# A gated S5 kernel: the head in two halves, a wider first weight block, and the square root table ahead of the loads

## The chip, the cores and the metric

The kernel runs on one core of a Trainium2 chip. The metric is the device time of one execution, in microseconds (us). The core has five engines that run their own instruction streams and wait for each other at semaphores: PE multiplies matrices (its weight loads are listed as PEld), DVE and ACT and POOL work element by element, and SP only issues transfers (DMAs). ACT and POOL can issue transfers too. A letter q behind an engine's name (SPq, ACTq) means its instruction queue.

## The reference, cut to what matters

The input x has 2048 tokens of 448 features. Two branches share one layer norm and are multiplied at the end.

```python
xn = layernorm(x)                                   # over the 448 features
# branch A: a diagonal complex state space scan over the tokens
dt = exp(log_dt); Lam_bar = exp(dt * Lam)
Bu = xn @ (((Lam_bar - 1) / Lam)[:, None] * Bmat).T
h[t] = Lam_bar * h[t-1] + Bu[t]
s = 2 * real(h @ Cmat.T) + xn * Dskip
# branch B: gated unit, 448 -> 1792 -> 448
hb = sigmoid(xn @ w_gate) * (xn @ w_up)
out = x + s * silu(hb @ w_down)
```

## The kernel before, in words

**Tiling.** The tokens are cut into four chunks of 512, and each chunk into four tiles of 128. Features lie on the partitions for the matmuls: `xnT` holds a chunk of normed tokens transposed, in seven slices of 64 features, doubled so that both halves of the partitions hold what they need. Gate and up weights (`wG`, `wU`) are loaded by halves of the partitions and by blocks of "steps". A chunk has 14 steps, seven of gate and seven of up. Each makes 256 columns (two groups of 128) for the chunk's tokens: seven pairs of matmuls on the upper and lower 64 rows (`gu_mm`, lines 653 and 654), in a `gu` buffer of two PSUM banks. There are three such buffers, used in turn. A gate step is emptied by a tanh on ACT (`gu_evac`, L667), an up step by a multiplication on DVE (L670).

**The scan.** It is turned into real arithmetic with tables of sines and cosines over the position in the chunk. `columns()` (L476) transposes four parameter vectors by small matmuls (L482, L484), copies them out (`pv`, L487), and makes from them `dt` (exp on ACT, L490), `theta` and `turn` on DVE (L499, L502, L504), `arg` (L499 as well) and `r` = exp(`arg`) on ACT (L507). `tables()` (L516) then switches ACT to the table set that has tanh, silu and sine (L518), after `dt` and `r`, and computes for each of four groups of states `v` (L522), `nu` (L525, L527), an absolute value (L530), a sine (L534) and a cosine (L536). Everything from L476 to here is issued in the planner's order, described below.

**The head.** Chunk 0 cannot use the transposes by DMA that the later chunks use, because all starts with it. For each of its tiles: two statistics instructions on DVE (`stats`, L387 and L388), the square root on ACT (L396), a cast of the mean on POOL (L397), the reciprocal (L398) and the norm (L410) on DVE, a copy of 64 columns on POOL (L414); then seven transposes on PE (`pe_transpose`, L439) and a copy to `xnT`: tile 0 by ACT and DVE (L443, L445), tile 1 by ACT (L451), tiles 2 and 3 by DVE (L448). Steps 0, 1 and 2 of gate are computed as tiles come: `g_head(lo, hi)` runs the three steps for tiles lo to hi only, that is with 128 tokens per matmul. The order on PE is that of the program: nine warm-up matmuls on zeros, transposes of tile 0, one warm-up, tile 1, one warm-up, steps 0 to 2 for tile 0, `columns()`, tile 2, the steps for tile 1, tile 3, the steps for tile 2, the steps for tile 3 with the tanhs, and then steps 3 to 13 over all 512 tokens.

**The loads.** SP and ACT issue them in program order (L326): x tiles 0 to 3 alternately, a first block of gate weights with two steps by each of the two queues, two parameter vectors each, on ACT the load of the square root table, then the second block of two steps by each, and on SP both halves of a third block with three steps, x tiles 4 to 7 in one transfer, and the up weights. The statistics of chunk 1 (`stats_for(1)`) read tiles 4 to 7.

**The order of the work.** Every operation is entered in a plan (`add`) with its engine, an assumed cost, and what it reads and writes. `solve` first gives PE's operations due times by adding costs in program order, with the first gate step not due before 5.9. It goes backward from there: each other operation gets a due time from what needs it and from what else its engine has to do. Then it goes forward with a clock of its own: whenever an engine is free, it takes, of the operations that are ready by then, the one with the earliest due time. A load is ready when a model of the transfers says so (all bytes one after another at a fixed rate). The instructions are emitted in the order of these starts, so the order on DVE, ACT and POOL is fixed when the kernel is built. Transfers, and all of PE, keep the program's order.

Of the kernel before, what the change touches and what calls it, by code (L numbers as in the profile page):

```python
# [14 lines left out]
ACT = mybir.ActivationFunctionType  # L15
# [57 lines left out]
class Plan:  # L73
# [8 lines left out]
    def add(self, eng, cost, fn, r=(), w=(), dma=0, lat=None, chain=False, name=""):  # L82
        o = Op()
        o.idx, o.eng, o.cost, o.fn, o.dma, o.name = len(self.ops), eng, cost, fn, dma, name
        o.lat = LAT.get(eng, 0.0) if lat is None else lat
        o.pre, o.suc = {}, []
        o.start = o.end = None
        for k in r:
            if k in self.w:
                self._edge(self.w[k], o, True)  # L90
        for k in w:
            for q in self.r.get(k, ()):
                self._edge(q, o, False)
            if k in self.w:
                self._edge(self.w[k], o, True)
        for k in w:
            self.w[k] = o
            self.r[k] = []
        for k in r:
            if k not in w:  # L100
                self.r.setdefault(k, []).append(o)
        if chain or eng == "PE":
            key = ("chain", eng)
            if key in self.last_of:
                self._edge(self.last_of[key], o, None)
            self.last_of[key] = o
        self.ops.append(o)
        return o
# [114 lines left out]
def kernel(  # L223
# [18 lines left out]
    V, A, G, T, Q = nc.vector, nc.scalar, nc.gpsimd, nc.tensor, nc.sync  # L242
# [8 lines left out]
    def flat(t, *dims):  # L251
        if len(dims) == 1:
            return t
        names = "abcd"[:len(dims)]
        kw = {n: v for n, v in zip(names[1:], dims[1:])}
        return t.rearrange("p (" + " ".join(names) + ") -> p " + " ".join(names), **kw)
# [63 lines left out]
    add = pl.add  # L320
# [3 lines left out]
    def load(eng, key, nbytes, o, i, cost=0.45, r=()):  # L324
        e = {"SP": Q, "ACT": A, "POOL": G}[eng]
        add(eng, cost, lambda: e.dma_start(out=o, in_=i), w=[key] if not isinstance(key, list) else key,  # L326
            r=r, dma=nbytes, chain=True)

    def load_x(t0, n, q="SP", r=()):
        load(q, [("x", t) for t in range(t0, t0 + n)], n * P * D * 2,  # L330
             x_all[:, t0:t0 + n, :], x_src[:, t0:t0 + n, :], r=r)

    BLK = {"g": [(0, 2), (2, 4), (4, 7)], "u": [(0, 3), (3, 7)]}

    def load_w(eng, k, half, b, r=()):
        m0, m1 = BLK[k][b]
        ps = slice(half * H, half * H + H)
        c0 = half * 896
        load(eng, [("w", k, half, m) for m in range(m0, m1)], H * 7 * (m1 - m0) * P * 2,
             wgt[k][ps, :, m0 * P:m1 * P],  # L340
             wsrc[k][:, c0 + m0 * P:c0 + m1 * P].rearrange("(s p) f -> p s f", p=H), r=r)
# [16 lines left out]

    for e in ("SP", "ACT", "POOL"):
        add(e, 0.7, lambda: None, chain=True)  # L360
    for t in range(4):
        load_x(t, 1, ("SP", "ACT")[t % 2])
    load_w("SP", "g", 0, 0)
    load_w("ACT", "g", 1, 0)
    for k, vec in enumerate((A_log_dt, A_Lambda_im, A_Lambda_re, A_Dskip)):
        load("ACT" if k < 2 else "SP", ("vrow", k), D * 2, vrow[k:k + 1, :], vec.unsqueeze(0), cost=0.25)
    add("ACT", 0.3, lambda: A.preload_act_table_set("sqrt_and_others"), w=["sqrttab"], lat=1.0, chain=True)
    load_w("SP", "g", 0, 1)
    load_w("ACT", "g", 1, 1)
    for h in range(2):  # L370
        load_w("SP", "g", h, 2)
    load_x(4, 4)
    for b in (0, 1):
        load_w("SP", "u", 0, b)
# [3 lines left out]
    def warm_mm(n):  # L378
        def f():
            for _ in range(n):  # L380
                T.matmul(gu[2][:, 0, :], lhsT=warm[:, 0:P], rhs=warm[:], start=True, stop=True)
        add("PE", (0.43 if n > 1 else 0.22) * n, f, r=["warm"], w=[("gu", 2)])
# [42 lines left out]
    def next_acc():  # L425
        a = acc_n[0] % 2
        acc_n[0] += 1
        return a
# [4 lines left out]
    def pe_transpose(t):  # L433
        b, a, js = t % NXN, next_acc(), slice(t * P, t * P + P)
        tp = flat(acc[a][:].bitcast(BF16)[:, 0:7 * P], 7, P)

        def f(s0, s1):
            for s in range(s0, s1):
                T.transpose(tp[:, s, :], xn[b][:, s * H:s * H + P], ident[:, :])  # L439
        add("PE", 0.36, lambda: f(0, 6), r=[("xn", b), "ident"], w=[("acc", a)])  # L440
        add("PE", 0.06, lambda: f(6, 7), r=[("xnw", b), ("xn", b), "ident", ("acc", a)], w=[("acc", a)])
        if t == 0:
            add("ACT", 0.476, lambda: A.copy(out=xnT[0][:, 0:4, js], in_=tp[:, 0:4, :]),  # L443
                r=[("acc", a)], w=[("xnT", 0, t, "a")])
            add("DVE", 0.27, lambda: V.tensor_copy(out=xnT[0][:, 4:7, js], in_=tp[:, 4:7, :]),  # L445
                r=[("acc", a)], w=[("xnT", 0, t, "b")])
        elif t > 1:
            add("DVE", 0.53, lambda: V.tensor_copy(out=xnT[0][:, :, js], in_=tp[:, :, :]),  # L448
                r=[("acc", a)], w=[("xnT", 0, t, "a"), ("xnT", 0, t, "b")])
        else:  # L450
            add("ACT", 0.9, lambda: A.copy(out=xnT[0][:, :, js], in_=tp[:, :, :]),  # L451
                r=[("acc", a)], w=[("xnT", 0, t, "a"), ("xnT", 0, t, "b")])
# [9 lines left out]
    def xr(c, lo=0, hi=TPC):  # L462
        return [("xnT", c % 3, j, h) for j in range(lo, hi) for h in "ab"]
# [174 lines left out]
    def next_gu():  # L638
        a = gu_n[0] % 3
        gu_n[0] += 1  # L640
        return a
# [3 lines left out]
    def gu_mm(c, k, m, a, lo, hi, first):  # L645
        x = xnT[c % 3]
        ts = slice(lo * P, hi * P)
        w_ = wgt[k]
        ms = slice(m * P, m * P + P)

        def f():
            for s in range(7):
                T.matmul(gu[a][:, 0, ts], lhsT=w_[0:H, s, ms], rhs=x[0:H, s, ts], start=(s == 0), stop=(s == 6))  # L653
                T.matmul(gu[a][:, 1, ts], lhsT=w_[H:P, (s + 1) % 7, ms], rhs=x[H:P, s, ts],  # L654
                         start=(s == 0), stop=(s == 6))
        n = (hi - lo) * P
        return add("PE", 7 * (0.0028 + n / 2400.0) + (2 * SW if first else 0), f,
                   r=xr(c, lo, hi) + [("w", k, 0, m), ("w", k, 1, m)], w=[("gu", a)], name=f"{k}{c}.{m}")
# [3 lines left out]
    def gu_evac(c, k, m, a):  # L662
        b = m % NSIG
        th, tk = (hF[1][:, m, :, :], ("hF", 1, m)) if c == 0 else (sig[b][:], ("sig", b))
        ho, hk = hF[c % 2][:, m, :, :], ("hF", c % 2, m)
        if k == "g":
            add("ACT", act(1024), lambda: A.activation(th, gu[a][:], ACT.Tanh, scale=0.5),  # L667
                r=[("gu", a)], w=[tk])
        else:
            add("DVE", dve1(1024), lambda: V.scalar_tensor_tensor(out=ho, in0=th, scalar=1.0, in1=gu[a][:],  # L670
                                                                 op0=ALU.add, op1=ALU.mult),
                r=[("gu", a), tk], w=[hk])
# [203 lines left out]
        norm(t)  # L876
    slots0 = [next_gu() for _ in range(3)]

    def g_head(lo, hi):
        for m in range(3):  # L880
            gu_mm(0, "g", m, slots0[m], lo, hi, m == 0)

    pe_transpose(0)
    warm_mm(1)
    pe_transpose(1)
    warm_mm(1)
    g_head(0, 1)
    columns()
    pe_transpose(2)
    g_head(1, 2)  # L890
    pe_transpose(3)
    g_head(2, 3)
    for m in range(3):
        gu_mm(0, "g", m, slots0[m], 3, 4, False)
        gu_evac(0, "g", m, slots0[m])
    b_load()
    def stats_for(c):
# [133 lines left out]
```

## Time and profile before

| what | value |
|---|---|
| median of three executions | 196.55 us (195.38 to 196.55) |
| the profiled execution | 195.65 us, of which span 193.9 us |
| granted PE clock, mean | 0.999 |
| busy: PE, DVE, ACT, POOL | 183.2, 161.8, 85.3, 38.6 us |
| transfers over the whole span | 13.31 MB, mean 69 GB/s |

The span runs from the first to the last instruction that the profiler records; the rest of an execution's time lies around it. A line of the profile names engine, line of the kernel, operation and tiles, with start and length in us. "Idle before" in square brackets is the time in which the engine did nothing, and behind the arrow stands what ended it. "Issue" is waiting for which the profile shows no cause. The chain of waits starts from the last instruction and is followed back, at each step to what released it. Matmuls overlap, so their lengths add up to more than the time that they take; the distance between their starts tells the pace.

### The profile page before, as it was taken

The page shows a single profiled execution, that of the slowest core. Times are in us where ns is not written, and L with a number is a line of the kernel's source. Part 1 is how long each engine was busy: PE and PEld are TensorE (multiplying, and loading weights), DVE is VectorE, ACT ScalarE, POOL GpSimd, SP SyncE. Part 2 cuts the span into 40 slices and gives each one's busy share as a digit, 9 for nine tenths or more (in the row PEclk, how much of TensorE's full clock was granted, in tenths as well). Part 3 has the DMA queues.
Part 4 walks back from the last instruction along what each step waited for, and adds up shares of the span by engine and source line. Part 5 has one row for each costly group of instructions (what it writes and reads, how often), then busy time and mean ns, then how long its engine had stood idle before and what let it go on. Part 6 is the DMA issues. An engine that isn't in the chain of part 4 may idle for free.

```text
span 193.9 us, 3710 instructions
## 1 busy us (share of the span) xinstructions
PE 183.2 (94%) x1482; PEld 91.3 (47%) x1489; DVE 161.8 (83%) x280; ACT 85.3 (44%) x120; POOL 38.6 (20%) x90
## 2 busy tenths in 40 slices
PE   7796999999999999999999999999989999999992
PEld 2583554444454454444445444444435444555561
DVE  3789678799999899999999999999997999540044
ACT  2757991745968652144467232334146421111110
POOL 4376843000008730000666100000000000000000
PEclk9999999999999999999999999999999999999999
DMA  5899975599300033200033410000000001010002
GB/s 140 220 249 222 127 166 74 112 333 206 111 0 0 3 71 78 44 0 0 0 31 93 98 44 3 24 0 27 24 24 0 3 0 46 9 45 24 0 26 70
DMA packets 30025, 13.31 MB, mean 69 GB/s; under 512 B 19636, under 2 KB 30008, under 8 KB 30008
## 3 DMA queue, kind: packets, MB, share of 16 engines
q1 hardware_dynamic: 28788, 12.39, 29.7%
q10 hardware_dynamic: 1220, 0.69, 1.4%
q8 instruction: 11, 0.18, 0.4%
q14 instruction: 6, 0.05, 0.1%
HBM read 6.66 MB, written 1.84 MB: 44 GB/s over the span
## 4 chain that ended last, share of the span: by engine, by line
DVE 49%; PE 33%; issue 6%; DMA 4%; POOL 3%; ACT 3%; ACTq 0%; DVEq 0%; POOLq 0%
PE gu L653 13%; DVE hF L670 11%; DVE wv L759 9%; PE acc L843 6%; PE gu L820 5%; PE acc L820 4%; DVE ta L752 3%; DVE tb L753 3%; DVE z L755 3%; DMA wG<-in_B_w_gate_dram 2%; DVE hT L776 2%; DVE ta L773 2%; DVE tb L774 2%; DVE o_t L856 2%; DVE wv L791 2%
## 5 line engine op out<-in xcount | busy, mean ns | idle before, releaser
L653 PE MATMUL gu<-xnT,wG 64*128 64x512 bf16 (+1 forms) x259 | 47.1, 324 | 2.7 <-issue 1.2
L654 PE MATMUL gu<-xnT,wG 64*128 64x512 bf16 (+1 forms) x259 | 47.2, 325 | 0.0
L653 PE MATMUL gu<-xnT,wU 64*128 64x512 bf16 x196 | 46.1, 376 | 0.0
L654 PE MATMUL gu<-xnT,wU 64*128 64x512 bf16 x196 | 46.1, 376 | 0.0
L667 ACT ACTIVATE sig<-gu 128x1024 f32<-128x1024 f32 x21 | 21.5, 1022 | 37.4 <-PE gu L654 37.4
L820 PE MATMUL acc<-wd,hF 128*128 128x448 bf16 x168 | 33.8, 353 | 0.0
L820 PEld LDWEIGHTS <-hF 128*128 128x128 bf16 x224 | 21.5, 98 | 21.3 <-issue 2.1
L653 PEld LDWEIGHTS <-wG 64*128 64x128 bf16 x259 | 20.8, 94 | 21.7 <-issue 2.5
L653 PEld LDWEIGHTS <-wU 64*128 64x128 bf16 x196 | 18.0, 94 | 23.0 <-issue 2.1
L670 DVE SCALAR_TENSOR_TENSOR hF<-sig,gu 128x1024 bf16<-128x1024 f32 x21 | 25.3, 1208 | 0.8 <-PE gu L654 0.8
L843 PE MATMUL acc<-cT,hT 128*128 128x448 bf16 x105 | 24.3, 353 | 0.0
L759 DVE TENSOR_TENSOR_SCAN wv<-c_r,st,z 128x512 bf16<-128x512 f32 x18 | 22.9, 1277 | 0.0
L856 DVE TENSOR_TENSOR o_t<-acc,g_t 128x448 bf16<-128x448 f32 x15 | 9.2, 616 | 16.3 <-PE acc L843 16.3
L654 PEld LDWEIGHTS <-wG 64*128 64x128 bf16 x259 | 20.5, 94 | 2.9 <-issue 2.7
L716 ACT CAST bus<-gu 128x1024 bf16<-128x1024 f32 x12 | 12.1, 1008 | 13.5 <-PE gu L705 10.9
L654 PEld LDWEIGHTS <-wU 64*128 64x128 bf16 x196 | 18.0, 94 | 0.0
L705 PE MATMUL gu<-xnT,bT 128*128 128x512 bf16 x65 | 15.3, 379 | 1.1 <-issue 1.1
L401 POOL TENSOR_SCALAR veb<-mv 128x2 bf16<-128x2 bf16 x6 | 4.2, 693 | 52.0 <-DVE st L769 27.4
L843 PEld LDWEIGHTS <-hT 128*128 128x128 bf16 x119 | 10.4, 98 | 7.3 <-issue 0.4
L826 ACT ACTIVATE g_t<-acc 128x448 bf16<-128x448 f32 x12 | 6.5, 540 | 14.8 <-PE acc L820 14.7
L387 DVE BATCH_NORM_STATS2 bst<-x_all 128x6 f32<-128x448 bf16 x16 | 9.5, 615 | 2.6 <-DMA x_all<-in_A_x_dram 2.6
L820 PE MATMUL gu<-wd,hF 128*128 128x448 bf16 x56 | 10.8, 352 | 0.0
(131 smaller groups left out, 244.5 us busy)
## 6 DMA issues: line engine op xcount, KB each, us to landing
out_dram<-o_t SPq DMA_DIRECT2D x15, 112.0 KB, 1.7
wd<-in_B_w_down_dram SPq DMA_DIRECT2D x1, 1568.0 KB
x_all<-in_A_x_dram SPq DMA_DIRECT2D x3, 448.0 KB, 5.0
wU<-in_B_w_up_dram SPq DMA_DIRECT2D x2, 448.0 KB, 11.3
wG<-in_B_w_gate_dram SPq DMA_DIRECT2D x2, 336.0 KB, 5.1
wU<-in_B_w_up_dram SPq DMA_DIRECT2D x2, 336.0 KB
wG<-in_B_w_gate_dram SPq DMA_DIRECT2D x2, 224.0 KB, 4.8
wG<-in_B_w_gate_dram ACTq DMA_DIRECT2D x2, 224.0 KB, 4.7
```

Of the source, the lines that this page charges most:

```text
L387: add("DVE", 0.53, lambda: V.bn_stats(out=bst[b][:], in_=x_all[:, t, :]), r=[("x", t)], w=[("bst", b)])
L653: T.matmul(gu[a][:, 0, ts], lhsT=w_[0:H, s, ms], rhs=x[0:H, s, ts], start=(s == 0), stop=(s == 6))
L654: T.matmul(gu[a][:, 1, ts], lhsT=w_[H:P, (s + 1) % 7, ms], rhs=x[H:P, s, ts], start=(s == 0), stop=(s == 6))
L667: add("ACT", act(1024), lambda: A.activation(th, gu[a][:], ACT.Tanh, scale=0.5), r=[("gu", a)], w=[tk])
L670: add("DVE", dve1(1024), lambda: V.scalar_tensor_tensor(out=ho, in0=th, scalar=1.0, in1=gu[a][:], op0=ALU.add, op1=ALU.mult), r=[("gu", a) ...
L705: T.matmul(gu[a][:, i, :], lhsT=bT[:, kt, i, pt * P:pt * P + P], rhs=x[:, 2 * kt, :], start=False, stop=(kt == 2))
L716: add("ACT", act(1024), lambda u=u, a=a: A.copy(out=bus[u][:], in_=gu[a][:]), r=[("gu", a)], w=[("bus", u)])
L759: dve(1.194, lambda k=k: V.tensor_tensor_scan(out=wv[:, k, :], data0=rb, data1=z[:, k, :], initial=(st[pt][:, k, :] if c else 0.0), op0=AL ...
L820: T.matmul(d, lhsT=hF[c % 2][:, m, h, js], rhs=wd[:, ft, :], start=(ft == 0), stop=(ft == FT - 1))
L826: add("ACT", act(448), lambda: A.activation(g_t[g][:], d, ACT.Silu, scale=0.5), r=[key, "silutab"], w=[("gt", g)])
L843: T.matmul(y, lhsT=hT[c % 2][:, hm, js], rhs=cT[:, cm, c0:c1], start=(i == 0), stop=(i == 6))
L856: add("DVE", dve1(n), lambda od=od, y=y, c0=c0, c1=c1: V.tensor_tensor(out=od, in0=y, in1=g_t[g][:, c0:c1], op=ALU.mult), r=[key, ("gt", g ...
```

## The change

Three edits, all in the head.

1. The blocks of the gate weights become (0, 3) and (3, 7) instead of (0, 2), (2, 4) and (4, 7). The loads of the third block go. The second block of each half is still issued by SP and ACT respectively, now with four steps.
2. The load of the square root table is entered ahead of all transfers, directly behind the start of ACT's chain, with an assumed cost of 0.05 and a latency of 1.5 (before: behind two parameter vectors, 0.3 and 1.0).
3. `g_head` goes. Steps 0, 1 and 2 are computed for tiles 0 and 1 together (256 tokens per matmul), with the transposes of tile 2 behind step 0, those of tile 3 behind step 1, and `columns()` between these and step 2. Then the three steps are computed for tiles 2 and 3 together, each with its tanh.

```diff
-    BLK = {"g": [(0, 2), (2, 4), (4, 7)], "u": [(0, 3), (3, 7)]}
+    BLK = {"g": [(0, 3), (3, 7)], "u": [(0, 3), (3, 7)]}
...
+    add("ACT", 0.05, lambda: A.preload_act_table_set("sqrt_and_others"), w=["sqrttab"], lat=1.5, chain=True)
     for t in range(4):
         load_x(t, 1, ("SP", "ACT")[t % 2])
     load_w("SP", "g", 0, 0)
     load_w("ACT", "g", 1, 0)
     for k, vec in enumerate((A_log_dt, A_Lambda_im, A_Lambda_re, A_Dskip)):
         load("ACT" if k < 2 else "SP", ("vrow", k), D * 2, vrow[k:k + 1, :], vec.unsqueeze(0), cost=0.25)
-    add("ACT", 0.3, lambda: A.preload_act_table_set("sqrt_and_others"), w=["sqrttab"], lat=1.0, chain=True)
     load_w("SP", "g", 0, 1)
     load_w("ACT", "g", 1, 1)
-    for h in range(2):
-        load_w("SP", "g", h, 2)
     load_x(4, 4)
...
-    def g_head(lo, hi):
-        for m in range(3):
-            gu_mm(0, "g", m, slots0[m], lo, hi, m == 0)
-
     pe_transpose(0)
     warm_mm(1)
     pe_transpose(1)
     warm_mm(1)
-    g_head(0, 1)
+    gu_mm(0, "g", 0, slots0[0], 0, 2, True)
+    pe_transpose(2)
+    gu_mm(0, "g", 1, slots0[1], 0, 2, True)
+    pe_transpose(3)
     columns()
-    pe_transpose(2)
-    g_head(1, 2)
-    pe_transpose(3)
-    g_head(2, 3)
+    gu_mm(0, "g", 2, slots0[2], 0, 2, True)
     for m in range(3):
-        gu_mm(0, "g", m, slots0[m], 3, 4, False)
+        gu_mm(0, "g", m, slots0[m], 2, 4, False)
         gu_evac(0, "g", m, slots0[m])
```

## The prediction

> **What bounds the kernel now.** I read the busy shares first, then the waits of the matrix engine (PE), then the chain of waits. The first two:
>
> ```profile
> PE 183.2 (94%) x1482; PEld 91.3 (47%) x1489; DVE 161.8 (83%) x280; ACT 85.3 (44%) x120; POOL 38.6 (20%) x90
> ```
>
> ```profile
> PE gu L653 <- issue: 1.2, 1, 1.2
> PE gu L381 <- DVE warm L347: 1.2, 1, 1.2
> ...
> PE gu L695 <- DVE hF L670: 0.6, 1, 0.6
> PE gu L653 <- ACT hF L667: 0.5, 1, 0.5
> ```
>
> PE is busy 94% of the span, and the only waits it has after 18.05 us are 0.6, 0.3 and seven switches of 0.16 us. What PE loses or gains before then moves the end by nearly the same amount. So I ask when PE starts gate step 3, the first with no part in the head. The chain of waits from 9.4 us on (start, length, what):
>
> ```profile
> 9.44 0.16 PE acc L482 x3
> 9.59 0.12 PE acc L484 x2
> 9.71 0.51 PE acc L439 x7
> ...
> 10.25 0.62 DVE xnT L448
> 10.88 0.08 DVE c_theta L499
> ...
> 12.37 0.08 DVE c_arg L499
> ...
> 12.47 0.20 ACT c_r L507
> ...
> 12.69 1.28 ACT L518
> ...
> 13.99 0.63 ACT spm L534
> 14.62 0.92 ACT hF L667
> ...
> 15.58 0.37 PE gu L653
> ```
>
> The reader should see that the head's matmuls are not what is late. Steps 0 to 2 fill all three `gu` buffers; step 3 needs the first one emptied by a tanh (L667), that needs the table load L518, that waits for `c_r` = exp(`c_arg`), and `c_arg` comes from `columns()`. The head's own matmuls end at 15.06. PE then waits 0.5 us, runs five of step 3's seven pairs, and stands still for 1.22 us in mid-step, waiting for nothing that the profile shows. The vector engine (DVE) around `c_arg`, in order of time:
>
> ```profile
> 12.28 0.15 DVE L499 TENSOR_TENSOR c_arg<-c_dt,pv 128x4 f32<-128x4 bf16 x1
> 12.40 0.74 DVE L527 SCALAR_TENSOR_TENSOR hT<-hT,hT 128x513 f32<-128x513 f32 x1
> 13.06 0.61 DVE L448 COPY xnT<-acc 128x896 bf16<-128x896 bf16 x1
> 14.13 1.15 DVE L387 BATCH_NORM_STATS2 bst<-x_all 128x6 f32<-128x448 bf16 x2 [0.46 <-DMA x_all<-in_A_x_dram]
> 15.20 0.30 DVE L388 BATCH_NORM_AGGREGATE mv<-bst 128x2 bf16<-128x6 f32 x2
> 15.42 1.12 DVE L387 BATCH_NORM_STATS2 bst<-x_all 128x6 f32<-128x448 bf16 x2
> ```
>
> `c_arg` stands before the four statistics of chunk 1, the first of which waits for the load of x tiles 4 to 7 until 14.13.
>
> **What the Trainium skill says.** (1) "Runtime: NRT & Kernel Launch", Instruction fetch mechanics: instructions are refilled in blocks of 16 KiB, 256 instructions, by a DMA queue of the sequencer. The trace agrees: queue q8 moves 11 packets, 0.18 MB. One is recorded at 15.2 us, beside loads that keep the DMA engines over 90% busy. I read the 1.22 us as a late block; that is an inference. (2) "TensorE: Matmul & The Clock Gate", Part 1: an array idle for a window of about 3.4 us drops to half clock, and needs about as long to recover; the windows are free-running. The trace shows the first half: nine warm-up matmuls 0.43 us apart, later pairs of the same width 0.216 apart. No gap of that length occurs after the warm-up (the longest is 0.9 us, before 6.10). (3) Same page and part: DVE is a strict FIFO. The trace agrees: the copy of tile 3 (13.06) follows the table operations though its transposes ended at 11.98. (4) "ScalarE: Activation LUTs", What ACT_TABLE_LOAD costs: 1283 ns, plus a drain of 1380. The trace shows 1.28 and no drain: the square root starts 0.02 after the load.
>
> **The change part by part.**
>
> *Square root table first.* The load leaves 3.74 to 5.02 us and lies ahead of the x loads. `mv` of tile 0 is there at 4.12, so the first reciprocal can follow `mv` of tile 1 at 4.77 instead of 5.37: norms and transposes of tiles 0 and 1 come 0.6 us earlier. ACT's queue now has it ahead of x1, x3, wG, two vectors and wG. Price: between 0.2 us (in the trace the next DMA issue follows the load's start by 0.20) and 1.28 (if issue waited for its end); not below zero, as nothing before it leaves. I take 0.2. It is hidden by the next item, as would be most of 1.28.
>
> *Weight block of three.* The first halves grow from 229 to 344 KB each. The old first blocks landed at 6.5, the second at 8.8 (wait of 0.41 ending 8.87): 459 KB in 2.3 us, 200 GB/s, so 229 KB more land at 7.65. The 0.41 goes. SP issues two DMAs less (0.62 each). The x load of tiles 4 to 7 follows the same bytes as before but larger pieces (768 and 1024 B instead of 512 and 768 B). Its bounds: 14.1 as now; 12.6, where DVE gets to it (below). wG in 512 and 768 B pieces moved 2065 KB from 1.9 to 12.0 us, 204 GB/s; wU in the larger ones runs at about 220 (13 to 15 us), which is 0.7 us less. I take 13.4.
>
> *The head.* Tile 1's copy (L451, 0.89) can end at 7.9; PE step 0 over 256 tokens runs 7.95 to 8.72 (seven pairs at 0.11, half of 0.216), transposes of tile 2 to 9.25, step 1 to 9.97, tile 3 to 10.5, `columns()` to 10.8, step 2 to 11.55, the second half 3 x 0.77 to 13.85. That is 1.2 us before the old 15.06, and 84 matmuls with 84 weight loads fewer. Worth nothing by itself: the tanh decides.
>
> *`columns()` moved behind tile 3 and step 1.* It ends at 10.8 instead of 9.7. DVE then copies tile 3 (10.55 to 11.17) and `pv` (11.3); `dt` 11.57, `theta` 11.6, `turn` twice, `v` of pair 0 at 12.15 to 12.6. Now the order. DVE's order is written by the planner: of the operations ready in its own clock the one with the earliest due time. Its numbers decide order alone; no time here is taken from them. Worked out of the kernel before by its rules, the due times are: statistics of tiles 4, 5 at 12.34, 12.87; `theta` 13.73, `v` 14.03, `nu` 14.43; statistics of 6, 7 at 14.83, 15.36; `c_arg` 15.89. Before, `columns()` was early enough that all of the `theta` group was placed (9.64 to 10.84 in planner time) ahead of x tile 4's landing there, 11.77. After, planner `theta` comes at 11.35 and `v` at 11.65, so at 12.05 the statistics are ready and more urgent. The new DVE order is `v`, statistics 4 and 5, `nu`, statistics 6 and 7, **then** `c_arg`. I worked this by hand from the listed costs; it is the step on which the forecast stands. Queued behind the first of them on DVE: everything to `c_arg`; who waits: `c_r`, table load, all tanh, PE.
>
> With x landing at T: statistics 4 and 5 with their aggregates 1.29 (14.13 to 15.42), `nu` 0.34, statistics 6 and 7 1.1, `c_arg` 0.15: T + 2.9. `c_r` 0.2, table 1.28: T + 4.4. The planner then takes tanh before the sine (due 10.3 against 21.2), 1.05 to PE's start: **T + 5.45**. For T = 13.4 PE starts step 3 at 18.85, 3.27 later than 15.58.
>
> *The late block.* The old stall came 20 PE instructions (five pairs, each two matmuls and two weight loads) behind the head. The head has 168 fewer, so that place in the stream moves 188 instructions, 47 pairs, 10.2 us of work, behind step 3's start, and PE has idled meanwhile: the block has time to come. I book −1.22; bounds −1.22 and 0.
>
> *Sum.* +3.27 − 1.22 = +2.05. On the way PE's waits of 0.6 and 0.3 could shrink, DVE's start of the scan waits for PE (1.66 us idle before 35.17), and chunk 1's transposes land about 36.5 against a need at 39.3, so neither absorbs nor adds. The profiled execution took 195.65 us (span 193.9 and 1.75 around it): 197.7. The runs shown have a median of 196.55, 0.9 higher; on that footing **198.6**.
>
> **The rivals.**
>
> *PE goes cold.* Same order, but PE idles from 13.85 to 18.85, 5.0 us, over the 3.4 of the skill's page; with free-running windows an estimate of the odds is (5.0 − 3.4)/3.4, a little under a half. Price from this trace: half rate for the 4.0 us that the warm-up took costs 2.0 us. 200.6. For it: the length of the gap. Against: no such gap in the trace.
>
> *Not slower: `c_arg` stays ahead of the statistics.* One mechanism with its place: DVE's order at `nu`. If the statistics come after, `nu` 12.6, `c_arg` 13.1, `c_r` 13.5, table 14.8, tanh to PE at 15.85: +0.27 − 1.22 = −0.95, 195.6; and with `c_arg` straight behind `theta` another 1.3 less, 194.3. It decides from the point where the planner has `c_arg` before x tile 4 lands. For it: `theta` misses that by only 0.4 of planner time. Against: `c_arg` is due after all four statistics.
>
> *The late block still comes*, elsewhere: 199.8. For it: the loads keep the DMA engines full until 21 us.
>
> **How the numbers follow.** Forecast 0.45, its own range 198.0 to 199.4 (T from 12.8 to 14.1); cold 0.33; late block 0.05; not slower 0.17 (0.12 near 195.6, 0.05 near 194.3). A measurement of this kernel can tell about 1% from no change, 1.97 us: slower begins at 198.5. That takes cold, the late block and 0.28 of the forecast: 0.66; within 1% 0.17 + 0.12 = 0.29; faster 0.05. The range 196.0 to 201.2 leaves out most of the not-slower case and the top of cold.
>
> **What would show it.** Right: on DVE `c_arg` stands behind four statistics and starts near 16.2; table load L518 near 16.5; PE idle before step 3 for about 5 us; no mid-step stall near 16.8. The first pair distances of step 3, 0.216 or 0.43, tell the clock. Wrong: `c_arg` before 13.5, or x tile 4 landing outside 12.6 to 14.1.

## The result, and the profile after

The changed kernel takes 201.67 us (median of four executions, 201.35 to 203.19) against 196.55 us (195.38 to 197.07) for the kernel before. The ratio is 1.0284, with a 95% interval of 1.0215 to 1.0354: slower, by 5.1 us where the forecast had 2.05, and above the forecast's range of 196.0 to 201.2. The profiled execution took 203.19 us (span 201.4), the longest of the four; its excess over the median, 1.5 us, is in what follows.

The busy shares after (busy us, share of the span, instructions), and PE's longest waits (us in all, times, longest), without the start of the warm-up and the switches of 0.16 us:

```profile
PE 186.1 (92%) x1398; PEld 91.8 (46%) x1405; DVE 161.4 (80%) x280; ACT 85.3 (42%) x120; POOL 37.5 (19%) x90
```

```profile
PE acc L437 <- DVE xn L408: 5.9, 1, 5.9
...
PE gu L693 <- ACT sig L665: 1.0, 1, 1.0
PE gu L651 <- ACT hF L665: 0.9, 1, 0.9
```

The 1.22 us stall on "issue" is gone. A new wait of 5.9 us has come, on the norm of tile 0 in front of the very first transposes, a place that the forecast had down as 0.6 us *earlier*. (Line numbers after the head are two lower than before.) The chain of waits after, from its beginning (start, length, what):

```profile
1.63 7.37 DMA wG<-in_B_w_gate_dram
...
9.03 0.23 ACTq L326
...
9.30 0.63 ACTq L326
...
10.03 0.30 ACT sdb L394
...
10.36 0.17 DVE rsd L396
```

ACT and its queue after, in order of time (start, length, engine, line, operation):

```profile
0.72 1.28 ACT L361 ACT_TABLE_LOAD   x1 [0.72 <-PEq L1009]
0.75 0.89 ACTq L326 DMA_DIRECT2D x_all<-in_A_x_dram  x2
1.67 0.71 ACTq L326 DMA_DIRECT2D wG<-in_B_w_gate_dram  x1
3.86 0.56 ACTq L326 DMA_DIRECT2D hF<-in_A_log_dt_dram  x1
9.03 0.23 ACTq L326 DMA_DIRECT2D hF<-in_A_Lambda_im_dram  x1
9.30 0.63 ACTq L326 DMA_DIRECT2D wG<-in_B_w_gate_dram  x1
10.03 0.48 ACT L394 ACTIVATE sdb<-mv,epsc 128x1 bf16<-128x1 bf16 x2 [8.03 <-DMA hF<-in_A_Lambda_im_dram]
```

and the same stretch of the kernel before, from `Lambda_im` on:

```profile
3.47 0.24 ACTq L326 DMA_DIRECT2D hF<-in_A_Lambda_im_dram  x1
3.74 1.28 ACT L367 ACT_TABLE_LOAD   x1 [3.74 <-DMA x_all<-in_A_x_dram]
3.94 0.61 ACTq L326 DMA_DIRECT2D wG<-in_B_w_gate_dram  x1
5.04 0.48 ACT L396 ACTIVATE sdb<-mv,epsc 128x1 bf16<-128x1 bf16 x2
```

The table is there at 2.0 us instead of 5.0. But the issue of `Lambda_im`, a vector of 0.9 KB, comes at 9.03 instead of 3.47. ACT takes its queue in order, so the second weight block and the square roots stand behind it, and the square roots come at 10.03 instead of 5.04.

Why that issue waits is in the listing of the built program, which names the completion semaphore that each instruction waits for. The loads use eight completion semaphores in turn, in the order of the listing, and each load first waits for the load that had its semaphore eight places earlier. ACT's part of both listings, shortened (`LoadActFuncSet` is the table load, DMAHW0 to DMAHW7 are the eight semaphores):

```
before  DMACopy x_all  128x448 x2
        DMACopy wG     64x7x256
        DMACopy log_dt 1x448
        DMACopy Lambda_im 1x448    [waits DMAHW0]    x tile 1 has it
        LoadActFuncSet
        DMACopy wG     64x7x256    [waits DMAHW3]
        Activation sdb
after   LoadActFuncSet
        DMACopy x_all  128x448 x2
        DMACopy wG     64x7x384
        DMACopy log_dt 1x448       [waits DMAHW1]    x tile 2 has it
        DMACopy Lambda_im 1x448    [waits DMAHW2]    SP's first weight block has it
        DMACopy wG     64x7x512    [waits DMAHW3]
        Activation sdb
```

The earlier table load shifts ACT's loads behind SP's in the planner's clock. SP's two x loads and its first weight block then come ahead of all of ACT's in the listing, and `Lambda_im` inherits the semaphore of that block, 344 KB instead of an x tile's 115.

PE, with nothing to do for 5.91 us, then runs its first work slowly. Its transposes and the first pairs of 256 tokens after:

```profile
11.10 0.93 PE L437 MATMUL acc<-ident,xn 128*128 128x128 bf16 x7 [5.91 <-DVE xn L408]
...
14.36 0.41 PE L651 MATMUL gu<-xnT,wG 64*128 64x256 bf16 x1
14.58 0.41 PE L651 MATMUL gu<-xnT,wG 64*128 64x256 bf16 x1
```

Seven transposes take 0.93 us (0.56 before), and the pairs are 0.215 us apart, the pace that twice as many tokens have later. Below, the array is called cold at this slow pace and warm at the full one. The slow pace lasts until about 20.3 us. Gate step 3 starts at 22.95 instead of 15.58, 7.37 later; without the old stall inside that step the difference is 6.15.

### The profile page after: what moved, and what is told of

It is laid out like the page before. It is cut to its first block, busy times and chain, and to the rows that moved or that the text cites. A ratio compares the mean times of both kernels' runs of the same rounds, so it can differ in the third digit from the quotient of the medians.

```text
span 201.4 us, 3539 instructions
## 1 busy us (share of the span) xinstructions
PE 186.1 (92%) x1398; PEld 91.8 (46%) x1405; DVE 161.4 (80%) x280; ACT 85.3 (42%) x120; POOL 37.5 (19%) x90
## 3 DMA queue, kind: packets, MB, share of 16 engines
HBM read 6.66 MB, written 1.84 MB: 42 GB/s over the span
## 4 chain that ended last, share of the span: by engine, by line
DVE 42%; PE 26%; POOL 8%; DMA 6%; SPq 6%; issue 5%; ACT 5%; ACTq 0%; DVEq 0%; POOLq 0%
DVE hF L668 9%; PE gu L651 7%; DVE wv L757 6%; PE acc L841 5%; PE gu L818 5%; SPq L344 5%; PE acc L818 4%; DMA wG<-in_B_w_gate_dram 4%; POOL nmr L403 3%; DVE ta L750 3%; DVE tb L751 3%; DVE z L753 2%; DMA xnT<-in_A_C_im_dram 2%; DVE ta L771 2%; DVE hT L774 2%
## 5 line engine op out<-in xcount | busy, mean ns | idle before, releaser
L651 PE MATMUL gu<-xnT,wG 64*128 64x512 bf16 (+1 forms) x217 | 48.2, 368 | 0.6 <-ACT xnT L449 0.6
L652 PE MATMUL gu<-xnT,wG 64*128 64x512 bf16 (+1 forms) x217 | 48.2, 368 | 0.0
L818 PE MATMUL acc<-wd,hF 128*128 128x448 bf16 x168 | 33.8, 353 | 0.0
L399 POOL TENSOR_SCALAR veb<-mv 128x2 bf16<-128x2 bf16 x6 | 3.1, 518 | 48.7 <-DVE st L767 25.6
```

Source lines behind the costliest of these rows:

```text
L818: T.matmul(d, lhsT=hF[c % 2][:, m, h, js], rhs=wd[:, ft, :], start=(ft == 0), stop=(ft == FT - 1))
```

## The experiments

One number makes all runs comparable: the start of PE's first matmul on B, the first work behind chunk 0's gate and up steps. Over all fourteen profiles the rest of the span, from there to the end, is between 161.7 and 162.8 us. So all but about 1 us of what a version wins or loses, it wins or loses ahead of that matmul. The ratio, to the kernel before measured beside it, comes from all executions of a run; starts and span come from the one that was profiled, which was up to 1.5 us longer than the median of its run (the changed kernel 1.5, e10 1.1, e11 1.0). Times in us.

| run | ratio, 95% interval | step 3 starts | first matmul on B | span |
|---|---|---|---|---|
| before | | 15.58 | 32.1 | 193.9 |
| after | 1.0284 [1.0215, 1.0354] | 22.95 | 39.2 | 201.4 |
| e1_table_back | 1.0009 [0.9981, 1.0037] | 15.85 | 32.9 | 195.7 |
| e2_table_only | 1.0207 [1.0121, 1.0293] | 20.21 | 37.0 | 198.8 |
| e3_table_behind_x | 1.0001 [0.9974, 1.0028] | 15.78 | 32.6 | 194.9 |
| e4_more_warm | 1.0153 [1.0073, 1.0233] | 18.30 | 35.0 | 196.9 |
| e5_head_only | 1.0010 [0.9986, 1.0034] | 14.45 | 32.1 | 194.3 |
| e6_block_only | 0.9988 [0.9953, 1.0024] | 15.82 | 32.0 | 193.9 |
| e7_nm_on_dve | 0.9956 [0.9929, 0.9982] | 14.55 | 31.7 | 193.8 |
| e8_act_freed | 0.9977 [0.9952, 1.0003] | 15.56 | 32.7 | 194.4 |
| e9_arg_pool | 1.0105 [1.0072, 1.0138] | 15.97 | 33.9 | 196.4 |
| e10_arg_nm | 1.0008 [0.9985, 1.0031] | 16.32 | 33.8 | 195.7 |
| e11_x4_arg_nm | 1.0048 [1.0028, 1.0068] | 19.20 | 34.3 | 196.2 |
| e12_bt_on_pool | 0.9954 [0.9927, 0.9981] | 15.15 | 31.2 | 192.9 |

### Which part of the change costs it

**e1: the change without the early table load.**

```diff
-    add("ACT", 0.05, lambda: A.preload_act_table_set("sqrt_and_others"), w=["sqrttab"], lat=1.5, chain=True)
     for t in range(4):
         load_x(t, 1, ("SP", "ACT")[t % 2])
...
+    add("ACT", 0.3, lambda: A.preload_act_table_set("sqrt_and_others"), w=["sqrttab"], lat=1.0, chain=True)
     load_w("SP", "g", 0, 1)
```

> The kernel after with its table load put back to its old place: head in halves and the block of three remain. Theory A (the loss comes from the table load at the front: it shifts which transfer shares a completion semaphore with which, so that the issue of the vector Lambda_im on ACT's queue waits for the first weight block, and the square roots stand behind it): first square root near 5.0 us, first transpose near 6.1, no wait of ACT until 9 us; as in the kernel after, the three tanh come ahead of c_r and the table load L516, so nothing holds step 3: it starts near 14.4 us and no mid-step stall follows. 194.0 to 195.0 us. Theory B (the head's new order costs, as forecast: tanh behind L516 behind four statistics): step 3 near 18.9 us, 198 to 199 us. Theory C (the halves themselves are slow): 200 or more.

**e2: the early table load alone, on the kernel before.**

```diff
+    add("ACT", 0.05, lambda: A.preload_act_table_set("sqrt_and_others"), w=["sqrttab"], lat=1.5, chain=True)
     for t in range(4):
         load_x(t, 1, ("SP", "ACT")[t % 2])
...
-    add("ACT", 0.3, lambda: A.preload_act_table_set("sqrt_and_others"), w=["sqrttab"], lat=1.0, chain=True)
     load_w("SP", "g", 0, 1)
```

> The kernel before with only the table load moved to the front. Theory A: Lambda_im waits for the first weight block of SP, here 229 KB, which lands near 6.5 to 7.5 us; first square root near 7.6 to 8.3, first transpose near 8.7 to 9.3, PE idle for 3.5 to 4 us and perhaps at half clock afterwards: 199 to 201 us, slower than before. Theory B or C: the front table load alone only brings the square root forward by 0.6 to 0.8 us: 195.5 to 196.6 us.

**e3: the change, with the table load behind ACT's two x loads instead of ahead of them.**

```diff
-    add("ACT", 0.05, lambda: A.preload_act_table_set("sqrt_and_others"), w=["sqrttab"], lat=1.5, chain=True)
     for t in range(4):
         load_x(t, 1, ("SP", "ACT")[t % 2])
+    add("ACT", 0.05, lambda: A.preload_act_table_set("sqrt_and_others"), w=["sqrttab"], lat=1.5, chain=True)
```

> The kernel after with the table load two instructions later on ACT: behind the loads of x tiles 1 and 3 instead of ahead of them. The order of the completion semaphores then has Lambda_im wait for an x tile, which has landed by 4. Theory A: first square root near 4.2 to 4.5 us, first transpose near 5.5, step 3 near 13.9, 193.3 to 194.5 us, at or below e1. Rival A2 (it is not the semaphore but the table load itself that holds ACT's queue for longer at the start): as the kernel after, 201 to 202 us. Theory B: 198 to 199 us.

Measured: e1 and e3 take what the kernel before takes; e2 alone is 2.1% slower. So the place of the table load makes nearly the whole loss. Theory A was right about the wait, but too hopeful about the rest: e1 took 196.91 us instead of 194.0 to 195.0 and e3 196.17 instead of 193.3 to 194.5, with step 3 at 15.85 and 15.78 instead of 14.4 and 13.9. The size of the block has a part in the loss. ACT's queue in e2, whose first blocks are 229 KB:

```profile
7.00 0.24 ACTq L326 DMA_DIRECT2D hF<-in_A_Lambda_im_dram  x1
...
8.00 0.48 ACT L396 ACTIVATE sdb<-mv,epsc 128x1 bf16<-128x1 bf16 x2 [6.00 <-DMA hF<-in_A_Lambda_im_dram]
```

The issue waits until 7.00 with a block of 229 KB. With one of 344 KB it waits until 9.03 in the changed kernel and until 7.68 in e4 (below), so the larger block adds between 0.7 and 2.0 us. In e3 the table is loaded early too, but in the listing the four x tiles stand ahead of the weight blocks again, and `Lambda_im` waits for an x tile (tile 3):

```profile
1.66 1.28 ACT L363 ACT_TABLE_LOAD   x1 [1.66 <-PEq L1009]
...
3.22 0.49 ACTq L326 DMA_DIRECT2D hF<-in_A_log_dt_dram  x1
4.03 0.23 ACTq L326 DMA_DIRECT2D hF<-in_A_Lambda_im_dram  x1
4.31 0.61 ACTq L326 DMA_DIRECT2D wG<-in_B_w_gate_dram  x1
5.03 0.48 ACT L394 ACTIVATE sdb<-mv,epsc 128x1 bf16<-128x1 bf16 x2 [2.09 <-DVE mv L386]
```

This settles two things. It is not the load of the table that costs, since here it is as good as first. And the table was not what the square roots waited for: with it ready at 2.9, they come at 5.03, behind ACT's own three issues, the last of which ends at 4.92. Before, the load at 3.74 to 5.02 lay beside those same issues. An early table therefore gains nothing by itself.

**e4: the change with 22 more warm-up matmuls, at the same assumed cost**, so that PE is busy while it waits and the planner's order stays.

```diff
-    def warm_mm(n):
+    def warm_mm(n, more=0):
         def f():
-            for _ in range(n):
+            for _ in range(n + more):
...
-    warm_mm(9)
+    warm_mm(9, 22)
```

> The kernel after with 22 more warm-up matmuls on zeros behind the nine, entered at the same assumed cost, so that nothing else moves: they fill most of PE's idle time from 5.2 to 11.1 us. Theory A with cold clock: the first transpose stays at 11.1, but the transposes take 0.56 instead of 0.93 us for seven and the 256-token pairs 0.11 instead of 0.215; step 3 near 20.0 instead of 22.95; 198.5 to 199.5 us. Rival (the clock is not what slows the head): pairs stay at 0.215, 201 to 202 us.

PE's first operations in e4:

```profile
1.17 8.44 PE L379 MATMUL gu<-warm 128*128 128x512 bf16 x31 [1.17 <-DVE warm L347]
9.78 0.56 PE L437 MATMUL acc<-ident,xn 128*128 128x128 bf16 x7 [0.17 <-DVE xn L408]
```

The transposes run at 0.56 again, and the ratio falls from 1.0284 to 1.0153, by 1.3% or 2.6 us. Not all of that is the pace. In the profile of e4 the weight block also landed earlier (`Lambda_im` at 7.68 instead of 9.03, the first transposes at 9.78 instead of 11.10), which these runs don't explain. Step 3 starts 4.65 us earlier: 1.3 come from that landing, and 3.3 from the pace (from the first transposes to step 3 it is 8.52 us in e4 and 11.85 in the changed kernel). The ratio holds both.

5.91 us without work is over the window of about 3.4 us that the Trainium skill, "TensorE: Matmul & The Clock Gate", Part 1, gives for an array to fall to half clock, so the trace fits the page. That the idle time was the cause is not shown: in e1 and e3 the first transposes were as slow (0.93 us) behind only 0.80 and 0.90 us of idle time. What e4 shows is that the slow pace goes when PE is kept busy. The time to recover differs from the page's, which the prediction took over as about as long as the window: here the slow pace lasted 9.2 us, from 11.10 to about 20.3, though PE never stood longer than 0.57 us in it.

### Where the head's gain went

e1 and e3 say that the rest of the change, taken alone, is worth nothing, though step 3 no longer stalls. (In both profiles the array was cold at first, which put step 3 some 1.3 us later; see the last section.) The next two runs take it apart.

**e5: the head in halves alone.** The diff is the third edit of the change on the kernel before.

> The kernel before with the head in two halves of 256 tokens and nothing else; blocks of two, two and three steps and the table load stay. My theory (the head is what shortens the start and removes the 1.2 us stall inside a gate step, and what brings ScalarE into the order in which the norm of chunk 1 stands ahead of a tanh): no stall between the start of gate step 3 and its end, ScalarE's three tanh ahead of the exponential of the time step's sine set, a PE wait of 1.0 to 2.0 us on a gate tanh between 25 and 33 us, and a time within 0.6 us of before, 195.8 to 197.0 us. Rival (the block of three, not the head, removes the stall): the stall of 1.2 to 1.5 us is still there, and the time is 196.5 to 198.0.

**e6: the blocks of three and four steps alone.** The diff is the first edit.

> The kernel before with only the gate's weight blocks of three and four steps instead of two, two and three; the head stays in four tiles of 128. My theory: the head's matmuls of the first tile wait longer for the larger block, so that gate step 3 starts 0 to 0.5 us later; the stall of 1.2 to 1.5 us inside a step remains, since the head has as many small matmuls as before; 196.3 to 197.3 us. Rival (the block removes the stall): no stall, step 3 of before's 15.6 us, 195.0 to 196.0 us.

The head removes the stall: e5 has none, e6 keeps one of 0.90 us and e2 one of 1.49 inside step 3. It also starts step 3 at 14.45, 1.13 us before the kernel before. Together 2.35 us, and yet the first matmul on B comes at 32.1 in both. The theory's wait on a gate tanh between 25 and 33 us is not there. PE waits for a gate tanh at 20 us and for an up product at 29, in e5:

```profile
20.06 0.37 PE L653 MATMUL gu<-xnT,wG 64*128 64x512 bf16 x1 [0.91 <-ACT hF L667]
29.13 0.37 PE L653 MATMUL gu<-xnT,wU 64*128 64x512 bf16 x1 [1.34 <-DVE hF L670]
```

And what stands before these two evacuations, on ACT and on DVE in e5:

```profile
14.63 1.15 DVE L387 BATCH_NORM_STATS2 bst<-x_all 128x6 f32<-128x448 bf16 x2 [1.36 <-DMA x_all<-in_A_x_dram]
...
17.29 0.14 DVE L499 TENSOR_TENSOR c_arg<-c_dt,pv 128x4 f32<-128x4 bf16 x1
...
27.43 0.39 DVE L598 COPY bT<-bT 64x896 bf16<-64x896 bf16 x1 [2.39 <-DMA bT<-in_A_B_im_dram]
27.85 2.35 DVE L670 SCALAR_TENSOR_TENSOR hF<-hF,gu 128x1024 bf16<-128x1024 bf16 x2
```

```profile
17.47 0.21 ACT L507 ACTIVATE c_r<-c_arg 128x4 f32<-128x4 f32 x1 [1.48 <-DVE c_arg L499]
17.69 1.28 ACT L518 ACT_TABLE_LOAD   x1
18.99 1.94 ACT L667 ACTIVATE hF<-gu 128x1024 bf16<-128x1024 f32 x2
```

Two loads hold the stretch. `c_arg` stands behind the statistics of x tiles 4 to 7, and `c_r`, the table load and the tanh of step 3 stand behind `c_arg`. Later a small copy of B waits 2.39 us for B's load, and the products that empty two up steps stand behind that copy. The second shows its weight only in e8 and e10; the theory that came first was another one.

**e7: the norm's product off GpSimd.** In e1 and e3 a multiplication of 128x2 numbers on POOL, in front of ACT's norm of tile 4, took 3.84 us (0.43 in the kernel before). e7 is e1 with this:

```diff
-        add("POOL", 0.4, lambda: G.tensor_tensor(out=nm, in0=mean, in1=rs, op=ALU.mult), r=ks("mv") + ks("rs"), w=ks("nm"))
-        add("POOL", 0.4, lambda: G.tensor_single_scalar(out=nm, in_=nm, scalar=-1.0, op=ALU.mult), r=ks("nm"), w=ks("nm"))
+        add("DVE", 0.15, lambda: V.scalar_tensor_tensor(out=nm, in0=mean, scalar=-1.0, in1=rs, op0=ALU.mult, op1=ALU.mult), r=ks("mv") + ks("rs"), w=ks("nm"))
```

> Head in halves and block of three with the table load in its old place, and for chunks 1 to 3 the product of mean and inverse deviation with the sign as one VectorE instruction instead of two on GpSimd. My theory (the gain of the head is given back because ScalarE, behind whose norm of tile 4 the tanh of a gate step stands, waits for a GpSimd multiply that lasts 3.84 us beside VectorE's table work): the PE wait on a gate tanh near 25 to 33 us falls from 1.5 - 1.7 to at most 0.5 us and the time to 194.5 to 195.6 us. Rival (the tanh is late for another reason, or the later waits take the gain): PE's waits on ScalarE up to 70 us still sum to over 2 us, and the time stays at 196.0 to 197.2 us.

The time is just above the theory's, 195.62 us, but not by its mechanism: PE still waits 1.86 us on a tanh, at 21.11, since here `c_arg` comes only at 18.35, behind x tiles that land at 15.5. Against the profile of e1, whose wait on a tanh was 1.74 us, two things went: a wait of 1.52 us at 57 us, and the cold array at the start (step 3 at 14.55 instead of 15.85). Which of them is in the ratio is not shown. The ratio to the kernel before is 0.9956, so e7 is faster by 0.2 to 0.7%.

**e8: ACT's queue freed.** As e7, with the table load as in e3, and

```diff
-        load("ACT" if k < 2 else "SP", ("vrow", k), D * 2, vrow[k:k + 1, :], vec.unsqueeze(0), cost=0.25)
+        load("SP", ("vrow", k), D * 2, vrow[k:k + 1, :], vec.unsqueeze(0), cost=0.25)
...
+    load_x(4, 4)
     load_w("SP", "g", 0, 1)
-    load_w("ACT", "g", 1, 1)
-    load_x(4, 4)
+    load_w("SP", "g", 1, 1)
```

> As the run with that VectorE product, but the table load directly behind ScalarE's two x loads, and all four vectors and both halves of the second gate block issued by SyncE, behind x tiles 4 to 7, so that ScalarE's queue holds nothing but its first three loads and the table before the square roots. My theory (what held the square roots in every run so far was ScalarE's own queue of transfer issues): first square root at 4.1 to 4.4 us instead of 5.0, first transpose 5.1 to 5.5 instead of 6.1, gate step 3 at 15.0 to 15.6 if the second block has landed, and 193.8 to 195.2 us. Rival (the square roots wait for the statistics or the table, or the later landing of the second block takes the 0.6 us back): gate step 3 not before 15.8, or a PE wait for weights of over 0.5 us, and the time within 0.5 us of the run with the VectorE product alone.

ACT's first square root in e8:

```profile
4.24 0.30 ACT L394 ACTIVATE sdb<-mv,epsc 128x1 bf16<-128x1 bf16 x1 [1.30 <-DVE mv L386]
```

The first square root comes at 4.24, as the theory had it: ACT's issues were the wait. The transposes follow at 5.48 instead of 6.1. The time did not follow (0.9977). x tiles 4 to 7 land at 10.3, so that their statistics now stand on DVE in front of the copies of tiles 2 and 3 and of `pv`; PE waits 0.75 and 0.59 for these copies, and 1.84 at 29.66 behind the same copy of B, which in this run waits 3.42 us for its load.

**e9: `c_arg` on GpSimd.** e1 with

```diff
-        small(tt(arg[:], dt_b[:], lre, ALU.mult), ["dt", "pv"], ["arg"])
+        pool(lambda: G.tensor_tensor(out=arg[:], in0=dt_b[:], in1=lre, op=ALU.mult), ["dt", "pv"], ["arg"])
```

> Head in halves, block of three, the table load in its old place, and the one small product of the time step with the real part of Lambda (c_arg) computed by GpSimd instead of by VectorE, where it stands behind the statistics of tiles 4 to 7. My theory (in all versions with the head in halves ScalarE's exponential c_r, the table load behind it and the tanh of all later gate steps wait until c_arg at 17.3 to 18.3 us, and ScalarE is full from there to about 29.5 us, which is where the head's gain goes): c_r at 13.0 to 14.5 us instead of 17.5, PE waits on ScalarE's or VectorE's evacuations up to 34 us at most 1.5 us in sum instead of 2.3, and the time 194.2 to 195.4 us. Rival (the norm of tile 4 sets the tanh behind it, whenever c_r comes): c_r early, but ScalarE stands again at 17 to 20.5 us until GpSimd's product for the norm is done, PE waits of 2 us or more remain, and the time is 195.7 to 196.8 us.

The rival is right, more than it asked for. `c_r` comes at 13.38, 4.4 us earlier than in e1, and ACT, having done four tanh, then stands. The norm of tile 4 on ACT in e9, and the product before it on POOL:

```profile
22.60 0.76 ACT L415 ACTIVATE xn<-x_all,nmr,rsd 128x448 bf16<-128x448 bf16 x1 [3.88 <-POOL nmr L403]
```

```profile
20.00 2.56 POOL L403 TENSOR_SCALAR nmr<-nmr 128x2 f32<-128x2 f32 x1
```

The tanh behind that norm holds PE for 2.13 us, and the kernel is 1.05% slower.

**e10: e9 and e7 together.**

> As the run before it, and the product of mean and inverse deviation for chunks 1 to 3 by one VectorE instruction as in the earlier run. My theory: c_r at 13.0 to 14.5 us; ScalarE's norm of tile 4 at or before 20.5 us; 193.8 to 195.2 us. Rival (the norm of tile 4 still waits for the statistics of tiles 4 and 5, whose x lands at 14.6 to 15.6 us): ScalarE idle over 1.5 us between 17 and 21 us, and 195.0 to 196.3 us.

`c_r` at 13.73, the norm of tile 4 at 19.71 and no idle stretch on ACT over 0.2 us from there to 29.7: the theory's steps hold, its time does not (1.0008). On DVE the copy of B has taken the place of the wait; DVE in e10:

```profile
29.06 0.39 DVE L595 COPY bT<-bT 64x896 bf16<-64x896 bf16 x1 [2.36 <-DMA bT<-in_A_B_im_dram]
29.48 1.22 DVE L667 SCALAR_TENSOR_TENSOR hF<-hF,gu 128x1024 bf16<-128x1024 bf16 x1
```

and PE waits 2.18 us at 30.76 for the product behind it.

**e11: e10 with x tiles 4 to 7 loaded ahead of the second weight block.**

```diff
+    load_x(4, 4)
     load_w("SP", "g", 0, 1)
     load_w("ACT", "g", 1, 1)
-    load_x(4, 4)
```

> As the run before it, and SyncE issues the load of x tiles 4 to 7 ahead of the second gate block, so that their statistics come early. My theory: x tiles 4 to 7 land at 10 to 11 us, c_r at 15.5 to 16.5 us, ScalarE busy without idle stretches over 0.7 us from 13 to 29 us, gate step 3 not later than 15.0, no PE wait for weights over 0.3 us, and the time 193.4 to 194.8 us, the best of all. Rival (the second gate block lands too late, or the up weights behind it do): a PE wait for wG or wU of over 0.5 us before 30 us, and 195 to 197 us.

Both theories fail at their first step. The planner believed the early landing and put the first statistic of tile 4 in front of the copy of tile 2; the tiles landed only at 13.3, and PE stood behind that copy. DVE in e11:

```profile
13.27 0.63 DVE L385 BATCH_NORM_STATS2 bst<-x_all 128x6 f32<-128x448 bf16 x1 [3.83 <-DMA x_all<-in_A_x_dram]
13.81 0.61 DVE L445 COPY xnT<-acc 128x896 bf16<-128x896 bf16 x1
```

PE's wait there is 3.17 us, and the kernel is 0.3 to 0.7% slower.

**e12: e10 with the copy of B on GpSimd.**

```diff
-        add("DVE", 0.53, lambda: V.tensor_copy(out=bT[0:H, 3, :, :], in_=bT[H:P, 3, :, :]),
+        add("POOL", 0.9, lambda: G.tensor_copy(out=bT[0:H, 3, :, :], in_=bT[H:P, 3, :, :]),
```

> As the run with c_arg on GpSimd and the norm's product on VectorE, and the copy of the last rows of the transposed B (64x896) done by GpSimd instead of by VectorE, where it stands ahead of a step's gate product and waits for the load of B. My theory (after ScalarE's wait is gone, what holds the stretch up to 30 us is VectorE, standing 2.4 us at that copy until B has landed at 26.6 to 29 us): no VectorE wait on the load of B, the PE wait of 2.2 us on VectorE's product near 30 us falls below 0.5 us, and the time is 193.6 to 195.0 us, below before's. Rival (the next work in order takes the place again: ScalarE is full until 29.7 us whatever comes earlier): VectorE's wait is gone but PE waits of 1.5 us or more on ScalarE or VectorE remain between 16 and 45 us, and the time is 195.3 to 196.8 us.

The wait for B's load now stands on POOL, where nothing urgent is behind it; the copy in e12:

```profile
27.80 0.99 POOL L595 COPY bT<-bT 64x896 bf16<-64x896 bf16 x1 [1.06 <-DMA bT<-in_A_B_im_dram]
```

PE's waits after the head, up to the first matmul on B, are 0.45 and 0.39 us, and that matmul comes at 31.2, the earliest of all runs. The ratio is 0.9954, with 194.95 us in its batch: better than the kernel before by 0.2 to 0.7%, and than e10, whose interval lies wholly above. (Of the 2.5 us by which that matmul is earlier than in e10's profile, 1.2 are there at step 3 already, where e10's array was cold at first; the wait of 2.18 us at 30.76 is what this edit took away.) Against the changed kernel it is about 3% better (0.9954 to 1.0284); against e7 no difference was measured.

## Why the prediction was wrong, step by step

- **"What PE loses or gains before 18 us moves the end by nearly the same amount": half right.** That the end follows the head holds, to about 1 us, for everything behind the first matmul on B (161.7 to 162.8 us in every run). But between 18 and 32 us there is a second limit, the loads of x tiles 4 to 7 and of B, seen through the order on ACT and DVE. A loss passes through it (7.37 us at step 3 of the changed kernel became 7.1 at the matmul on B), a gain does not (2.35 us in e5 became none).
- **"Square root table first: 0.6 us earlier; price between 0.2 and 1.28": this is the step that failed.** The price was the delay of one DMA issue, 5.6 us at that issue and 5.0 at the square root and the first transposes (11.10 instead of 6.10). The cold array added 3.3 us on the way to step 3, and the head in halves saved 1.0 (8.52 us from the first transposes to step 3 in e4, 9.48 in the kernel before): together the 7.37. I had priced the load by its own length on ACT's queue and not asked what the changed order does to the loads themselves. The cue was in the profile of before: ACT's table load there is marked as released by the DMA of an x tile, which it does not read; it stood behind `Lambda_im`, which waited for x tile 1's semaphore. The other half of the step failed too: the table was not the last thing that the square root waited for (e3).
- **Weight block of three, landing at 7.65:** the release of `Lambda_im` puts it at 9.0 in the changed kernel, 7.7 in e4. The 0.41 us wait for weights is gone, as forecast, in e1 and e3 too; but in e6, where the first step comes at 8.01, PE waits 0.58 us for the larger block. x tiles 4 to 7 were issued early (4.04) in the changed kernel and land at 12.9, within the bounds of 12.6 to 14.1; with the table elsewhere and their load in its old place they land at 14.6 to 15.5, outside them.
- **The head's matmuls end at 13.85:** 14.45 in e5, where step 3 follows them without a wait. Step 0 starts at 8.37 instead of 7.95, having waited 1.06 us for ACT's copy of tile 1, and the rest of the 0.6 is spread over the head.
- **DVE's order, "the step on which the forecast stands": right.** In every version with the head in halves in which DVE computes `c_arg`, it stands behind all four statistics: at 17.29 in e5, and in the changed kernel (DVE):

```profile
22.80 1.15 DVE L385 BATCH_NORM_STATS2 bst<-x_all 128x6 f32<-128x448 bf16 x2
23.86 0.15 DVE L497 TENSOR_TENSOR c_arg<-c_dt,pv 128x4 f32<-128x4 bf16 x1
```

- **"`c_r` 0.2, table 1.28, then tanh; PE's start T + 5.45": wrong for the steps that it was said of.** The tanh of steps 0 to 2 need no new table, and the planner puts them ahead of `c_r`. ACT after:

```profile
21.63 2.85 ACT L665 ACTIVATE hF<-gu 128x1024 bf16<-128x1024 f32 x3 [1.43 <-PE gu L652]
24.36 0.22 ACT L505 ACTIVATE c_r<-c_arg 128x4 f32<-128x4 f32 x1
24.59 1.28 ACT L516 ACT_TABLE_LOAD   x1
25.88 1.94 ACT L665 ACTIVATE hF<-gu 128x1024 bf16<-128x1024 f32 x2
```

  In the kernel before the tanh came behind that table load only because of the order there, and I took an order for a dependence. The 3.27 us were booked at the wrong place; what the late `c_arg` does cost is the wait of 0.91 us in e5 (1.86 in e7), three steps later.
- **The late block, −1.22: right**, and for the head alone (gone in e5, kept in e2 and e6; in none of the eleven profiles with the head in halves, in all three without). That it was a late block of instructions stays an inference that no run tests.
- **The rival of the cold array: wrong in its place, and near in its price by luck.** I gave the gap behind the head (5.0 us, which never came) and 2.0 us, half rate for 4.0 us. It came ahead of the head, beside 5.91 us of idle time, and lasted 9.2 us; in the profiles it cost 3.3. (The longest gap of the kernel before behind its warm-up is the stall of 1.22 us, not the 0.9 that I gave; both are far from 3.4.)
- **The rival of no loss:** its mechanism, `c_arg` ahead of the statistics, was made by hand in e9 and e10. It did not reach 195.6: the places behind it took the time.

The direction came out as forecast by luck, since the mechanism was not the one at work. Without the table's move the same reasoning would have said slower for a change that measures as none (e1, 1.0009).

## What to carry to other kernels

Before moving an instruction within a queue that also issues loads, list which completion semaphore each load takes and waits for, before and after: a tiny load can inherit the wait for a large one, and everything in order behind it pays. When PE starts earlier and nothing comes of it, look for the load whose landing a short instruction waits for in front of an evacuation, and move that short instruction to an engine with nothing urgent behind it. Such waits come one behind another, so make each removal show itself in the trace before the next.

## What the runs showed of the hardware that I had not expected

- **A multiplication of 128x2 numbers on POOL took 0.43 us in the kernel before, 2.56 in e9 and 3.83 or 3.84 in e1, e3, e4 and the changed kernel.** The long ones lie beside DVE's table operations, run back to back, and end with them. In the changed kernel it ran from 26.01 to 29.85, and DVE's operations from 25.39 to 29.76:

```profile
26.19 1.09 DVE L523 TENSOR_SCALAR hT<-hT 128x513 f32<-128x513 f32 x3
27.20 1.89 DVE L525 SCALAR_TENSOR_TENSOR hT<-hT,hT 128x513 f32<-128x513 f32 x3
29.00 0.76 DVE L528 TENSOR_SCALAR hT<-hT 128x513 int32<-128x513 int32 x2
```

  The Trainium skill, "SBUF — State Buffer", SBUF: two separate sides, says that DVE and POOL share one pair of ports, and that a POOL instruction and a DVE instruction of certain kinds (in a two-port mode, or with two inputs in SBUF) shut each other out of it for a whole instruction. The trace agrees in time, as if POOL had got no turn between these eight DVE instructions. But a row of them does not always keep POOL out. In the kernel before (POOL, then DVE):

```profile
19.59 1.05 POOL L402 TENSOR_TENSOR sdb<-veb,halfc 128x2 bf16<-128x2 bf16 x1
19.38 1.89 DVE L527 SCALAR_TENSOR_TENSOR hT<-hT,hT 128x513 f32<-128x513 f32 x3
```

  Here a POOL instruction began and ended within three DVE instructions in a row. What decides it is not shown: no run varied the DVE operations alone.
- **The array is not always warm after nine warm-up matmuls.** At 6 us the seven transposes took 0.56 us in the profiles of before, e5, e6, e7, e11 and e12 and 0.93 in those of e1, e3, e9 and e10, behind the same nine matmuls and an idle gap of 0.74 to 1.40 us in the first group and 0.8 to 0.91 in the second. Step 3 starts at 14.45 (e5) and 14.55 (e7) with a warm array, and at 15.78 (e3) and 15.85 (e1) with a cold one, 1.3 us apart, from the same head. What decides it was not tried. The granted clock of the record does not tell the two apart: from 11 to 20.3 us, in the slow stretch of the changed kernel, its mean is 1.00.
